# A convolution and spectral-mixing kernel: x kept on chip, mixing with stationary weights, and the kept part added in phase 3

## The chip, the cores and the metric

The kernel runs on one core of one Trainium2 chip. A core has a matrix engine (TensorE, PE in the profile, whose weight loads are listed as PEld), a vector engine (VectorE, DVE), a scalar engine (ScalarE, ACT), a general engine (GpSimd, POOL), a queue engine (SyncE, SP) and 16 DMA engines that move data between DRAM and the on-chip memory SBUF. Matrix results land in a second on-chip memory, PSUM. The metric is the device time in microseconds of one execution.

## The reference

The input x has 8 batches of 3264 positions with 192 channels, in float32. First comes a causal convolution with 7 taps, whose taps are a softmax and are shared by the 24 channels of each of 8 heads. Its result u0 goes through a spectral mixing of 64 modes, and a dense layer ends it:

```python
w = exp(weight - weight.max(-1)); w = w / (w.sum(-1) + 1e-9)
u0 = einsum('hk,bskhg->bshg', w, windows_of_7(x))
X = rfft(u0, axis=1)
Yr = einsum('bmd,mde->bme', Xr, w_r) - einsum('bmd,mde->bme', Xi, w_i)
Yi = einsum('bmd,mde->bme', Xr, w_i) + einsum('bmd,mde->bme', Xi, w_r)
y = irfft(Yr + 1j * Yi, n=S, axis=1)
u = u0 + y
out = u + maximum(u @ w_ch, 0.0)
```

Only the first 64 modes of Y are filled. w_r and w_i are 64 x 192 x 192 each.

## The kernel before

The sequence is cut into 27 windows of 122 output positions; a window needs 128 input positions (6 overlap), one per partition. `load_xw` (L73 to L81) fetches one batch into `xw` as bf16 with three DMAs that POOL issues; three such buffers exist, so batch b+2 is fetched when batch b-1 has been used.

Setup: the taps' softmax (L87 to L106), the band matrices `cband` from seven masks made by POOL (L114) and 56 DVE steps (L120, L125), and the table of cosines and sines `fstore` from a chain on DVE over 1728 elements per partition (`kprod` L144, `targ` L153 to L160) and two sines on ACT (L164, L166).

Phase 1, per batch: `conv_loop` (L300) runs, for each window and head, one matmul with the window as the stationary side (32 columns) and the band as the moving side (122 columns), L318. The result comes out transposed, channels on partitions. DVE copies four windows at a time to `cTA` and `cTB` (L329, L331), which hold the convolved sequence of all batches. `dft_and_correction` (L338) multiplies `fstore` with the unconvolved x (L343), and turns that into the spectrum of the convolved sequence by further small matmuls (L360, L363) with the operators `rop` and `cgm`; two transposes (L368, L369) and eight strided DVE copies put it into `xtA` and `xtB`.

Then 27 transposes of `fstore`, scaled by ACT, give the inverse table `gstore` (L434, L435). Mixing (L444 to L503): for each of 8 groups of 8 modes four DMAs on POOL fetch the weights (L450; two buffers of each). The spectrum is the stationary side (32 columns) and the weights are the moving side (192 columns), L479; the result is copied to `ymix` (L486), transposed (L487, L488) and copied to `yeT` (L492, L498).

`zwi` (L515 to L517) multiplies the mixed spectrum with [w_ch, identity], 384 columns. Phase 3 (L522 to L549), for each of 208 tiles of up to 128 positions: three matmuls with 384 columns accumulate [u @ w_ch, u]: L533 and L535 from the stored convolution with [w_ch, identity] (`wi`), L537 from `gstore` and `zwi`. ACT takes the Relu of the first half (L540), DVE adds the second half (L541), and SP sends three tiles with one DMA (L544; L549 for the two last tiles of a batch). `otile` has three buffers.

The framework inserts the semaphores. A buffer is reused only when its last reader is done, DMAs included. Each engine works through its own stream in order, and these streams are ordered when the program is built.

## Time and profile before

| | us |
|---|---|
| median of 3 runs (345.3 to 348.7) | 347.3 |
| span of the profiled execution | 344.8 |
| PE busy | 261.6 |
| DVE busy | 243.2 |
| ACT busy | 85.7 |
| POOL busy | 73.7 |

The profiled execution's own time is not listed apart from its span, the time from its first to its last instruction. A row of a group reads: line, engine, operation, output <- inputs, partitions x elements and type, count | busy us, mean ns of one | idle time of the engine before them and what ended it. A row of the timeline reads: start, length, engine, line, operation. "Granted clock" is the share of full TensorE clock that the chip allowed, and a DMA's time to landing runs from its issue to the arrival of its last byte. Two neighbouring matmuls overlap, so the distance of two starts is their price, not the length of one.

### The profile page before, as it was taken

To read this page: it belongs to the slowest core of one execution; us is meant where nothing else is said; L and a number is where in the kernel's file an instruction comes from. 1 tells how busy PE (TensorE), PEld (TensorE's weight loads), DVE (VectorE), ACT (ScalarE), POOL (GpSimd) and SP (SyncE) were. 2 spreads that over 40 slices of the span, in tenths; PEclk is the share of its full clock that TensorE was granted. 3 is DMA by queue.
4 is the path that set the end of the run, shared out by engine and by line. 5 is a ranking of instruction groups with operands and counts; after the bars stand their busy time and mean duration, and the time that the engine had idled before them with its cause. 6 is when DMAs were issued, how large, how long until landed. Compare 5 with 4: busy or idle time off the path is not lost.

```text
span 344.8 us, 7813 instructions
## 1 busy us (share of the span) xinstructions
PE 261.6 (76%) x3075; PEld 147.0 (43%) x3075; DVE 243.2 (71%) x700; ACT 85.7 (25%) x246; POOL 73.7 (21%) x116
## 2 busy tenths in 40 slices
PE   0232283776787895694489899889899999999985
PEld 0121251554555664431133333325465565565552
DVE  3999999999979998420064754665577676676654
ACT  3000310000000000024400000005566666666653
POOL 8869303732133000000163333000000000000000
PEclk9999999699899987655555555557999999999999
DMA  8930914999959900000099999203555555555554
GB/s 91 191 37 10 140 16 49 191 191 156 151 58 132 129 3 2 0 2 0 0 153 158 164 162 155 34 0 102 186 178 190 196 192 195 190 191 191 199 177 155
DMA packets 81172, 40.68 MB, mean 118 GB/s; under 512 B 55024, under 2 KB 81136, under 8 KB 81136
## 3 DMA queue, kind: packets, MB, share of 16 engines
q0 software_dynamic: 53600, 20.10, 50.6%
q1 hardware_dynamic: 27536, 20.09, 17.3%
q8 instruction: 24, 0.39, 0.5%
q14 instruction: 12, 0.10, 0.1%
HBM read 40.21 MB, written 20.05 MB: 175 GB/s over the span
## 4 chain that ended last, share of the span: by engine, by line
PE 43%; DVE 24%; issue 20%; DMA 7%; POOL 4%; ACT 1%; POOLq 0%; DVEq 0%; ACTq 0%
PE gps L533 9%; PE mixt L479 9%; PE gps L537 8%; PE gps L535 8%; DVE cTB L331 5%; DMA out_dram<-otile 4%; DVE cTA L329 4%; DVE cband L125 3%; DMA wiB<-in_moe_w_i_dram 2%; PE xps L343 1%; PE blk_a L318 1%; PE et L488 1%; DVE ymix L486 1%; PE et L487 1%; POOL xw L77 1%
## 5 line engine op out<-in xcount | busy, mean ns | idle before, releaser
L541 DVE TENSOR_TENSOR otile<-rz,gps 128x192 f32<-128x192 f32 x208 | 72.9, 353 | 35.7 <-ACT rz L540 8.4
L540 ACT ACTIVATE rz<-gps 128x192 f32<-128x192 f32 x208 | 68.6, 330 | 101.9 <-PE gps L537 100.1
L533 PE MATMUL gps<-wi,cTA 128*128 128x384 bf16 x208 | 69.0, 332 | 2.6 <-DVE otile L541 2.5
L537 PE MATMUL gps<-zwi,gstore 128*128 128x384 bf16 x208 | 68.6, 330 | 0.0
L535 PE MATMUL gps<-wi,cTB 128*128 128x384 bf16 x208 | 68.6, 330 | 0.0
L318 PEld LDWEIGHTS <-xw 128*32 128x32 bf16 x1728 | 32.7, 106 | 69.0 <-issue 62.6
L318 PE MATMUL blk_a<-cband,xw 128*32 128x122 bf16 x864 | 30.0, 244 | 35.5 <-DVE cband L125 14.6
L486 DVE CAST ymix<-mixt 16x192 bf16<-16x192 f32 x64 | 22.3, 352 | 31.1 <-PE mixt L479 29.2
L318 PE MATMUL blk_b<-cband,xw 128*32 128x122 bf16 x864 | 28.9, 243 | 18.4 <-DVE cTB L331 12.0
L329 DVE CAST cTA<-blk_a 128x488 bf16<-128x488 f32 (+1 forms) x56 | 36.2, 647 | 1.1 <-PE blk_a L318 1.1
L435 ACT ACTIVATE gstore<-tpsg,ascale 128x122 bf16<-128x122 bf16 (+1 forms) x27 | 9.8, 362 | 106.9 <-PE tpsg L434 106.9
L331 DVE CAST cTB<-blk_b 128x488 bf16<-128x488 f32 (+1 forms) x56 | 35.0, 626 | 0.1
L343 PE MATMUL xps<-xw,fstore 128*128 128x192 bf16 x216 | 30.0, 285 | 0.7 <-DVE fstore L168 0.7
L533 PEld LDWEIGHTS <-cTA 128*128 128x128 bf16 x208 | 20.6, 99 | 17.8 <-issue 5.7
L535 PEld LDWEIGHTS <-cTB 128*128 128x128 bf16 x208 | 20.7, 99 | 16.2 <-issue 4.3
L537 PEld LDWEIGHTS <-gstore 128*128 128x128 bf16 x208 | 20.7, 99 | 13.8 <-issue 0.7
L450 POOL DMA_DIRECT2D wrA<-in_moe_w_r_dram x8 | 7.2, 901 | 84.8 <-PE mixt L479 81.5
L343 PEld LDWEIGHTS <-fstore 128*128 128x128 bf16 x216 | 19.9, 111 | 5.8 <-issue 1.1
L479 PE MATMUL mixt<-wrA,xtA 128*32 128x192 bf16 x64 | 16.6, 333 | 5.1 <-DVE ymix L486 3.3
L479 PE MATMUL mixt<-wrB,xtB 64*32 64x192 bf16 x64 | 16.9, 341 | 0.0
L479 PEld LDWEIGHTS <-xtB 64*32 64x32 bf16 x128 | 8.4, 100 | 19.0 <-issue 18.8
L479 PEld LDWEIGHTS <-xtA 128*32 128x32 bf16 x128 | 8.6, 102 | 16.3 <-issue 12.0
(126 smaller groups left out, 286.5 us busy)
## 6 DMA issues: line engine op xcount, KB each, us to landing
out_dram<-otile SPq DMA_DIRECT2D x64, 288.0 KB, 2.3
xw<-in_x_dram POOLq DMA_DIRECT2D x8, 1200.0 KB, 11.2
wrA<-in_moe_w_r_dram POOLq DMA_DIRECT2D x8, 384.0 KB, 5.7
wiA<-in_moe_w_i_dram POOLq DMA_DIRECT2D x8, 384.0 KB, 7.7
wrB<-in_moe_w_r_dram POOLq DMA_DIRECT2D x8, 192.0 KB, 6.0
wiB<-in_moe_w_i_dram POOLq DMA_DIRECT2D x8, 192.0 KB, 7.7
out_dram<-otile SPq DMA_DIRECT2D x8, 96.0 KB, 2.1
out_dram<-otile SPq DMA_DIRECT2D x8, 48.0 KB, 1.9
```

Of the source, the lines that this page charges most:

```text
L125: nc.vector.scalar_tensor_tensor(out=cband[:, h, :], in0=maskk[:, k, :], scalar=wsb[:, h, k:k + 1], in1=cband[:, h, :], op0=ALU.mult, op1= ...
L318: nc.tensor.matmul(tconv[32 * g : 32 * g + 32, col0 : col0 + WIN], xw[:, c, xc0 : xc0 + 32], cband[:, h, :], start=True, stop=True, tile_p ...
L329: nc.vector.tensor_copy(out=cTA[:, b, s_begin : s_begin + blk_cols], in_=blk_a[:, 0:blk_cols])
L331: nc.vector.tensor_copy(out=cTB[:, b, s_begin : s_begin + blk_cols], in_=blk_b[:, 0:blk_cols])
L343: nc.tensor.matmul(xps[:, 0:D], fstore[:, c, :], xw[:, c, :], start=(c == 0), stop=(c == NWIN - 1))
L479: nc.tensor.matmul(tls[pos][r, 0:D], stat, wst[:, mj, :], start=(pi == 0), stop=(pi == len(plan) - 1), tile_position=(0, 32 * pos))
L486: nc.vector.tensor_copy(out=ymix[r, :], in_=tls[pos][r, 0:D])
L533: nc.tensor.matmul(gps[0:ns, 0:2 * D], cTA[:, b, si:si + ns], wi[:, 0, :], start=True, stop=False)
L535: nc.tensor.matmul(gps[0:ns, 0:2 * D], cTB[:, b, si:si + ns], wi[:, 1, :], start=False, stop=False)
L537: nc.tensor.matmul(gps[0:ns, 0:2 * D], gstore[:, si:si + ns], zwi[:, b, :], start=False, stop=True)
L540: nc.scalar.activation(out=rz[0:ns, :], in_=gps[0:ns, 0:D], func=ACT.Relu)
L541: nc.vector.tensor_tensor(out=otile[0:ns, t, :], in0=rz[0:ns, :], in1=gps[0:ns, D:2 * D], op=ALU.add)
```

## The change

The kernel body is rewritten.

- All of x is loaded once into `x_all` (all batches, bf16): 24 DMAs of 8 or 9 windows and one each for the first and last window of all batches, all on POOL. `perm`, a signed permutation, is built on POOL behind the loads.
- The bands: softmax on 8 partitions, the taps written to a zeroed row, the row sent to DRAM (`vdram`) and read back as 128 shifted copies, reversed by one DVE copy.
- `conv_unit`: the band is the stationary side (128 columns), up to 10 windows of one head the moving side (216 columns on average), 24 matmuls per batch. ACT copies each half of the heads over x itself in `x_all`, 48 copies in all.
- `dft` multiplies the table with the convolved sequence, so the correction, `rop`, `cgm` and `ccrm` are gone. `xtrans` transposes the 64-mode spectrum, real and imaginary parts stacked on the partitions, by six small matmuls.
- The convolved sequence is also transposed into `cT`: `t_part` makes up to 8 blocks of 122 positions in PSUM and DVE copies them at once; 6 parts per batch, 48 in all. 28 are issued in phase 1, 20 in the mixing, one per group.
- Mixing: 32 groups of 2 modes, five buffers of weights, two DMAs per group (real parts to partitions 0 to 63, imaginary to 64 to 127). The weights are the stationary side (128 columns), the spectrum the moving side (16 columns), 384 matmuls. The result has the channels on partitions already; no transposes follow.
- Phase 3: 54 groups of two windows and two batches (the last windows of four batches for two of them), 12 matmuls each: four with 384 columns, eight with 192. The Relu argument accumulates in `z`; `y` holds only the mixed part. VectorE adds the convolved sequence from `x_all` to `y`, and a second add of the Relu runs on GpSimd for two groups of three and on VectorE for the third. Four DMAs on SP send a group. `r` and `t` have three buffers each.

The trig chain is the same but for its base, and `yeT` and `zwi` (now in four pairs, scaled there) have the same use.

```diff
...
+    UNITS = ((0, 10), (10, 8), (18, 9))
+    USLOTS = ((0, 15), (15, 12), (27, 14))
...
+    x_all = constp.tile([P, B, NWIN, D], BF16, tag="x_all")
...
+    def load_mid(b, c0, n):
+        nc.gpsimd.dma_start(out=x_all[:, b, c0:c0 + n, :], in_=xwin_src(b, c0, n))
+    lastrow0 = WIN * (NWIN - 1) - OV
+    nlast = S - lastrow0
+    nc.vector.memset(x_all[0:32, :, 0, :], 0.0)
+    nc.vector.memset(x_all[96:P, :, NWIN - 1, :], 0.0)
+    load_mid(0, 1, 9)
+    nc.gpsimd.dma_start(out=x_all[OV:P, :, 0, :], in_=x[:, 0:WIN, :].rearrange("b p d -> p b d"))
+    load_mid(0, 10, 8)
+    nc.gpsimd.dma_start(out=x_all[0:nlast, :, NWIN - 1, :],
+                        in_=x[:, lastrow0:S, :].rearrange("b p d -> p b d"))
+    load_mid(0, 18, 8)
...
+    vdram = dramp.tile([H, 256], BF16, name="vdram")
...
+        nc.vector.tensor_scalar(out=vrow[:, 127:127 + KK], in0=wexp[:], scalar1=wrec[:, 0:1],
+                                scalar2=None, op0=ALU.mult)
+        nc.sync.dma_start(out=vdram[:], in_=vrow[:])
+        va = vdram[:]
+        hank = sp.tile([P, H, P], BF16, tag="hank")
+        nc.sync.dma_start(out=hank[:], in_=bass.AP(tensor=va.tensor, offset=va.offset,
+                                                   ap=[[1, P], [256, H], [1, P]]))
+        nc.vector.tensor_copy(out=cband[:], in_=hank[:, :, ::-1])
...
+    for b in range(1, B):
+        load_mid(b, 1, 9)
+        load_mid(b, 10, 8)
+        load_mid(b, 18, 8)
+    nc.gpsimd.memset(perm[:], 0.0)
+    nc.gpsimd.affine_select(out=perm[:, 0:64], in_=perm[:, 0:64], compare_op=ALU.not_equal, fill=-1.0,
+                            base=-64, pattern=[[-1, 64]], channel_multiplier=1)
...
+    wp = early_stack.enter_context(tc.tile_pool(name="wts", bufs=5, side="right"))
+    wtiles = []
+    for g in range(NGRP):
+        wt = wp.tile([P, MG, 3, D], BF16, tag="wt")
+        for half, src in ((0, moe_w_r), (1, moe_w_i)):
+            nc.gpsimd.dma_start(out=wt[64 * half:64 * half + 64, :, :, :],
+                                in_=src[MG * g:MG * g + MG, :, :].rearrange("m (p j) e -> p m j e", j=3))
+        wtiles.append(wt)
...
+    def conv_unit(b, u):
+        w0, n = UNITS[u]
+        for half in range(2):
+            cp = pconv.tile([P, 4, 256], F32, tag="cv")
+            for j in range(4):
+                h = 4 * half + j
+                nc.tensor.matmul(
+                    cp[:, j, 0:GRP * n].rearrange("p (w e) -> p w e", w=n), cband[:, h, :],
+                    x_all[:, b, w0:w0 + n, GRP * h:GRP * h + GRP], start=True, stop=True)
+            dst = x_all[0:WIN, b, w0:w0 + n, 96 * half:96 * half + 96].rearrange(
+                "p w (j e) -> p j w e", j=4)
+            srcv = cp[0:WIN, :, 0:GRP * n].rearrange("p j (w e) -> p j w e", w=n)
+            nc.scalar.copy(out=dst, in_=srcv)
...
+    def t_part(b, s0, n):
+        tp = ptr.tile([P, 8 * WIN], BF16, tag="tp")
+        for k in range(n):
+            t_slot(tp[:, WIN * k:WIN * k + WIN], b, s0 + k)
+        nc.vector.tensor_copy(out=cT[:, b, WIN * s0:WIN * (s0 + n)], in_=tp[:, 0:WIN * n])
+    def dft(b):
+        xp = pxx.tile([P, 512], F32, tag="xp")
+        for c in range(NWIN):
+            k = WIN if c < NWIN - 1 else LASTVALID
+            nc.tensor.matmul(xp[:, 0:D], fst[0:k, c, :], x_all[0:k, b, c, :],
+                             start=(c == 0), stop=(c == NWIN - 1))
...
+    def xtrans(b, xs):
+        tp = pxx.tile([P, 3, P], F32, tag="xt")
+        xsv = xs[:, :].rearrange("k (p j) -> k j p", j=3)
+        for j in range(3):
+            nc.tensor.matmul(tp[0:64, j, :], xsv[:, j, :], ident[:], start=True, stop=True,
+                             tile_position=(0, 0))
+            nc.tensor.matmul(tp[64:P, j, :], xsv[:, j, :], perm[:], start=True, stop=True,
+                             tile_position=(0, 64))
...
+    tq = []
+    pend = None
+    for b in range(B):
+        for u in range(3):
+            conv_unit(b, u)
+            if u == 0 and b > 0:
+                pend = (b - 1, dft(b - 1))
+            if u == 1 and pend is not None:
+                xtrans(*pend)
+                pend = None
+            if b < 5:
+                for _ in range(2):
+                    if tq:
+                        t_part(*tq.pop(0))
+            tq.extend(t_unit_halves(b, u))
+    xtrans(B - 1, dft(B - 1))
...
+        wt = wtiles[g]
+        for mj in range(MG):
+            m = m0 + mj
+            for t in range(2):
+                o = yps[:, t, 16 * (m % HALF):16 * (m % HALF) + 16]
+                for j in range(3):
+                    nc.tensor.matmul(o, wt[:, mj, j, 64 * t:64 * t + P], xt[:, j, m, :],
+                                     start=(j == 0), stop=(j == 2))
...
+        if gq and g % 2 == 0:
+            g_part(gq.pop(0))
+        if tq:
+            t_part(*tq.pop(0))
+    while tq:
+        t_part(*tq.pop(0))
+    early_stack.close()
+    ps1.close()
...
+    p3 = ctx.enter_context(tc.tile_pool(name="p3", bufs=3, side="right"))
+    pz = ctx.enter_context(tc.tile_pool(name="pz", bufs=2, space=PSUM))
...
+    def group(combos):
+        zp = pz.tile([P, 2, 512], F32, tag="z")
+        yp = pz.tile([P, 2, 512], F32, tag="y")
+        for k, (q, w) in enumerate(combos):
+            sa, sb, par = slot_of(w)
+            glhs = gst[:, WIN * w:WIN * w + P]
+            nc.tensor.matmul(zp[:, k, 0:2 * D], glhs, zwi[:, 0, 2 * q:2 * q + 2, :], start=True, stop=False)
+            for i in range(2):
+                b = 2 * q + i
+                o = zp[:, k, D * i:D * i + D]
+                nc.tensor.matmul(o, cT[:, b, WIN * sa:WIN * sa + P], win0[:, 0:D], start=False, stop=False)
+                nc.tensor.matmul(o, cT[:, b, WIN * sb:WIN * sb + P], wBs[par], start=False, stop=(i == 1))
+            nc.tensor.matmul(yp[:, k, 0:2 * D], glhs, zwi[:, 1, 2 * q:2 * q + 2, :], start=True, stop=True)
+        last = combos[0][1] == NWIN - 1
+        n = LASTVALID if last else WIN
+        r = p3.tile([P, 2, 2 * D], F32, tag="r")
+        t = p3.tile([P, 2, 2 * D], F32, tag="t")
+        nc.scalar.activation(out=r[0:n, :, :], in_=zp[0:n, :, 0:2 * D], func=ACT.Relu)
+        q0, w0 = combos[0]
+        tv = t[0:n, :, :].rearrange("p k (b e) -> p k b e", b=2)
+        yv = yp[0:n, :, 0:2 * D].rearrange("p k (b e) -> p k b e", b=2)
+        if last:
+            xv = x_all[0:n, 2 * q0:2 * q0 + 4, w0, :].rearrange("p (k b) e -> p k b e", k=2)
+        else:
+            xv = x_all[0:n, 2 * q0:2 * q0 + 2, w0:w0 + 2, :].rearrange("p b k e -> p k b e")
+        nc.vector.tensor_tensor(out=tv, in0=yv, in1=xv, op=ALU.add)
+        npool[0] += 1
+        eng = nc.gpsimd if npool[0] % 3 else nc.vector
+        eng.tensor_tensor(out=t[0:n, :, :], in0=t[0:n, :, :], in1=r[0:n, :, :], op=ALU.add)
+        if last:
+            dst = out[2 * q0:2 * q0 + 4, WIN * w0:WIN * w0 + n, :].rearrange("b p e -> p b e")
+            nc.sync.dma_start(out=dst, in_=t[0:n, :, :].rearrange("p k (b e) -> p (k b) e", b=2))
+        else:
+            for i in range(2):
+                dst = out[2 * q0 + i, WIN * w0:WIN * (w0 + 2), :].rearrange("(k p) e -> p k e", k=2)
+                for r0, r1 in ((0, 112), (112, WIN)):
+                    nc.sync.dma_start(out=dst[r0:r1], in_=t[r0:r1, :, D * i:D * i + D])
...
+    zwi_pair(0)
+    for q in range(B // 2):
+        for i in range(PAIRS):
+            group([(q, 2 * i), (q, 2 * i + 1)])
+            if i == 1 and q + 1 < B // 2:
+                zwi_pair(q + 1)
+        if q % 2 == 1:
+            group([(q - 1, NWIN - 1), (q, NWIN - 1)])
...
```

606 lines of the change are left out of this document (147 added, 459 removed).

## The prediction

> **What bounds the kernel now.** I read the cores first, then the busy time by stage, then the groups and the timeline.
>
> ```profile
> core 0: 344.8 us, clock 0.837
> 0.00:12.40 12.40, 0.00 (x0) 0.00 (x0) 6.50 (x30) 2.81 (x3) 11.26 (x29) 1.00 1.04 121
> 12.40:142.00 129.60, 82.60 (x2102) 59.22 (x2102) 121.85 (x314) 4.54 (x8) 43.52 (x64) 0.92 0.78 91
> 142.00:171.00 29.00, 17.59 (x80) 6.74 (x80) 4.99 (x17) 9.77 (x27) 0.00 (x0) 0.54 0.00 1
> 171.00:225.00 54.00, 48.46 (x254) 18.72 (x253) 32.11 (x126) 0.00 (x0) 18.87 (x24) 0.50 1.15 132
> 225.00:232.20 7.20, 6.91 (x16) 1.65 (x16) 4.28 (x10) 0.00 (x0) 0.00 (x0) 0.50 0.00 0
> 232.20:344.80 112.60, 106.05 (x625) 60.67 (x624) 73.50 (x209) 68.61 (x208) 0.00 (x0) 0.98 0.53 179
> ```
>
> The columns are the stretch, its length, the busy time of PE, weight loads, DVE, ACT and POOL, then granted clock, DMA share and GB/s. Each stage has its own limit. The convolution (12.4 to 142) is DVE's, 121.85 of 129.6 us. From 142 to 171 nothing is full: PE and ACT pass 27 transposes of gstore to each other one by one, and the DMA engines rest. The mixing (171 to 225) is held by PE at clock 0.50 while its weights arrive alongside. The last stage is PE's, 106 of 112.6 us. So the question is what each stage is bound by next.
>
> ```profile
> 276.00 0.33 PE L533 MATMUL gps<-wi,cTA 128*128 128x384 bf16 x1
> 276.98 0.33 PE L533 MATMUL gps<-wi,cTA 128*128 128x384 bf16 x1
> 80.72 1.66 PE L343 MATMUL xps<-xw,fstore 128*128 128x192 bf16 x18
> 100.34 0.36 PE L363 MATMUL xcps<-xs,rop 128*128 128x24 bf16 x8
> 142.09 0.23 PE L368 MATMUL xtps<-ident,xcs 128*128 128x128 bf16 x1 [0.45 <-DVE xcs L366]
> 142.25 0.24 PE L369 MATMUL xtps<-ident,xcs 128*64 128x128 bf16 x1
> 8.00:16.00 8.00, 1.41 (x37) 1.13 (x41) 8.00 (x31) 0.00 (x0) 7.71 (x23) 1.00 1.60 191
> 176.00:186.00 10.00, 9.06 (x48) 3.63 (x47) 5.05 (x20) 0.00 (x0) 3.77 (x5) 0.50 1.59 190
> ```
>
> These price PE and the loads. Between the two L533 rows lie six matmuls of 384 columns: 0.98/6 = 163 ns each. Of the 18 with 192 columns the last ends some 0.25 us after its start: (1.66-0.25)/17 = 83 ns. That makes 0.417 ns per column plus 3, the weight load hidden: 93 ns for 216 columns, 54 for 122. Eight with 24 columns and a full stationary side take (0.36-0.17)/7 = 27 ns each. The two isolated transposes start 160 ns apart, load not hidden. Loads saturate at 190 GB/s as bf16, x and mixing weights alike.
>
> **Start: the convolution begins at 16 us instead of 12.4.** The 56 DVE steps that built the bands go; the bands now travel to DRAM and back between the softmax and one reversing copy.
>
> ```profile
> 5.51 0.22 DVE L103 TENSOR_TENSOR wsb<-wexp,wrec 128x56 f32<-128x56 f32 x1
> 243.94 4.36 DMA out_dram<-otile
> out_dram<-otile SPq DMA_DIRECT2D x8, 48.0 KB, 1.9
> wiA<-in_moe_w_i_dram POOLq DMA_DIRECT2D x8, 384.0 KB, 7.7
> 22.30 1.94 DVE L144 TENSOR_TENSOR kprod<-sidx,midx 128x1728 f32<-128x1728 f32 x1
> 24.17 0.65 DVE L329 CAST cTA<-blk_a 128x488 bf16<-128x488 f32 x1
> 24.75 1.04 DVE L153 TENSOR_SCALAR targ<-kprod 128x1728 f32<-128x1728 f32 x1
> ```
>
> Softmax ends at 5.7. Each hop costs between 1.9 (smallest transfer of the output) and 7.7 (loaded queue); I take 4.4, an output landing under load. The copy of 1024 elements costs 1.2 at kprod's rate. 5.7+8.8+1.2 = 15.7; ends 10.7 and 22.3. The trig chain is unchanged. The last two rows show that DVE's stream is ordered by readiness (a copy of the convolution stands between two trig steps written ahead of it), so I let trig fill DVE while the bands travel.
>
> **Phase 1: PE 16 to 85 us.**
>
> ```profile
> L329 DVE CAST cTA<-blk_a 128x488 bf16<-128x488 f32 (+1 forms) x56 | 36.2, 647 | 1.1 <-PE blk_a L318 1.1
> L331 DVE CAST cTB<-blk_b 128x488 bf16<-128x488 f32 (+1 forms) x56 | 35.0, 626 | 0.1
> ```
>
> The 112 evictions leave DVE (36.2+35.0 = 71 us), and so do 64 strided copies to xtA and xtB. New on PE: convolution 8x24x93 ns = 17.9; dft 8x27x83 = 17.9; xtrans 48x160 = 7.7; transposes 55 per batch, 28 of the 48 parts here, so 257. Each is 54 (hidden load) to 160 ns (isolated); I take 80, nearer the hidden end since equal shapes follow each other as in the xps row: 20.6, ends 13.9 and 41.1. Sum 64, hence 80.
>
> ```profile
> L540 ACT ACTIVATE rz<-gps 128x192 f32<-128x192 f32 x200 | 66.0, 330 | 99.7 <-PE gps L537 97.9 <-DVE otile L541 1.8
> L164 ACT ACTIVATE fstore<-targ2a 128x1728 bf16<-128x1728 f32 x1 | 1.6, 1643 | 28.0 <-DVE targ2a L160 28.0
> L351 DVE COPY cct<-ccps 6x256 bf16<-6x256 bf16 x8 | 2.1, 264 | 0.0
> POOL wi L252 <- DMA xw<-in_x_dram: 3.5, 1, 3.5
> ```
>
> Beside it: ACT's slope is (1643-330)/1536 = 0.855 ns per element, so a half of 864 elements takes 0.9; 48 of them and the two sines make 46, done near 62. DVE copies 976 elements in 1.0 (L351 four times) to 1.3 (L329 twice): 28 to 36 us for 28 parts and 16 of trig. x is 10.5 MB at 190 GB/s from 4 us: all here by 59. None ends after 80. One wait is new: perm is built on POOL behind 24 loads of x, and the L252 row is POOL's thirteenth DMA held until an earlier one landed, the fifth by count. So if POOL keeps eight in flight, it frees when the eighteenth of 26 lands, 7.2 MB or 42 us, and xtrans of batch 0, with all later PE work behind it, can stand for 0 to 15 us. I add 5: 85.
>
> **Phase 2: 85 to 132.** The 29 us of gstore alone vanish (4 transposed blocks ride in the mixing), as do ymix, its zeroing and the yeT transposes. 384 matmuls at 27 ns are 10 us, 20 parts at 9.2x80 ns are 15: PE has room at full clock. The bytes stay 9.4 MB. Five of 32 groups are fetched ahead; 27x295 KB/190 = 41.9, plus 1.4 before the first refill is issued (group 0 and two issues of 0.56, next row) and about 3.5 to land, mix and copy the last group: 47. Stationary weights buy little here by themselves.
>
> ```profile
> L279 POOL DMA_DIRECT2D winat<-in_moe_w_ch_dram x1 | 0.6, 555 | 0.0
> ```
>
> By the 0.50 of the mixing stage with PE busy 48 of 54 us, PE could run this stage at half clock: transposes 160, matmuls 54 ns, 54 us in sum, 7 more. The Trainium skill (TensorE: Matmul & The Clock Gate, Part 4) says that transposes do not count as PE work for the gate; by that rule half clock holds here and the sum ends 7 us later. The 0.54 in the transposing stage agrees, but idle PE would explain that too.
>
> **Phase 3: 134.3 to 243.7.** The first zwi pair costs 4x0.43+0.56 = 2.3 (6.91/16 from the table). A group of 488 rows then costs PE 4x163+8x83 = 1.32 us, and there are 54: 71 us against 106. But its results pass through one of three t buffers.
>
> ```profile
> L541 DVE TENSOR_TENSOR otile<-rz,gps 128x192 f32<-128x192 f32 x200 | 70.3, 354 | 34.3 <-ACT rz L540 6.9 <-DMA out_dram<-otile 4.5
> 7.99 1.62 POOL L114 TENSOR_SCALAR_AFFINE_SELECT maskk<-ones_f 128x122 f32<-128x122 f32 x6
> L272 POOL MEMSET winat<- 128x768 bf16 x1 | 0.7, 737 | 0.1
> 15.13 0.35 POOL L254 TENSOR_SCALAR_AFFINE_SELECT wi<-wi 24x192 bf16<-24x192 bf16 x1
> 20.55 3.90 POOL L254 TENSOR_SCALAR_AFFINE_SELECT wi<-wi 24x192 bf16<-24x192 bf16 x1
> L544 SPq DMA_DIRECT2D out_dram<-otile x64: 372/372/402, 236.1 to 340.5; - x64
> ```
>
> VectorE add of 768: 354+576x(1940-354)/1536 = 0.95. Second add, two of three times on POOL, which no row shows: six selects of 122 elements in 1.62 are 2.2 ns per element, 1.70 for 768; ends 0.74 (memset of the same size) and, scaled from L254, 15.6. I take 1.70, the f32 row. Then four DMAs on SP at 0.37: the last starts 1.11 later and lands after 1.9. With 0.2 for the hops a buffer comes free after 0.95+1.70+1.11+1.9+0.2 = 5.86, and three groups need it: 1.95 per group. SP alone needs 1.49, DVE 0.95+0.32 = 1.27, POOL 1.13, ACT 0.82. So the buffers set the pace, PE waits, and phase 3 takes 54x1.95 = 105.5, no better than before; waits for t already show in L541's row. The last group ends 3.9 after the pace: 134.3+105.5+3.9 = 243.7.
>
> **Sum.** 16+69+47+2.3+105.5+3.9 = 243.7 against the span of 344.8; the median of the runs shown is 347.3, 2.5 above that span: **246 us**.
>
> **Rivals.** (a) The buffers return sooner: POOL's add at the memset's 0.74 gives 4.9/3 = 1.63 per group, 88 us, total 229; SP's 1.49 is the floor, 221. For it: fixed costs inside the select's row. Against: two inputs per element. (b) PE lags: transposes at 160 ns and the full wait for perm put phase 1 at 16+85+15 = 116, and half clock adds 7: 284. For it: the isolated transposes and the L252 wait. Against: hidden loads at equal shapes. (c) Slower than before: POOL is locked out by VectorE. The select of 3.90 us ran beside kprod and the last band steps on DVE; its like took 0.35. Phase 3 would need 206.6 us for no change, so 36 POOL adds above 5.7 us each decide it; at 15.6 the kernel takes about 700. Against: only every third group has a VectorE add with two SBUF inputs. The Trainium skill (SBUF — State Buffer, Who interferes with whom) makes just such instructions, and the two-port modes, lock GpSimd out; the slow select beside steps of those kinds agrees. By it the lock costs at most one 0.95 per three groups, 17 us in all.
>
> **How the numbers follow.** My forecast 0.50 (its own range 228 to 262), (a) 0.22, (b) 0.20, (c) 0.04, another way 0.04. The range of 8 in 10 reaches from (a)'s floor with phase 1 a little early, 214, to (b), 286. A measurement of this kernel tells about 1% from no change: faster 0.94, within 1% 0.02, slower 0.04.
>
> **What would show it.** Convolution at 16; the last xtrans near 85; load rate 190 GB/s without a gap through the mixing; in phase 3 VectorE's first add waiting for an output DMA in most groups, PE at two thirds, groups 1.95 us apart. Groups 1.5 apart with SP always issuing would be (a); PE busy at clock 0.5 before 100 us would be (b); POOL full in phase 3, (c). A POOL add far from 1.70 or a PE stream that waits for perm breaks the sum first.

## The result and the profile after

The kernel takes 309.1 us (median of 4 runs, 305.9 to 310.9) against 348.0 for the kernel before in the same comparison: a ratio of 0.887, 95% interval 0.878 to 0.896. The sign was right. The time, 246 with a range of 214 to 286, was not. Some executions take 1 to 2% longer than the fastest of their kernel; the ratios leave these out, and the profile of the run with five t buffers, four r buffers and four batches is of such an execution (287.3 us). First the busy time by stage of the changed kernel; the columns are those of the table before.

```profile
core 0: 308.0 us, clock 0.847
0.00:26.70 26.70, 0.00 (x0) 0.00 (x0) 9.02 (x17) 1.49 (x2) 13.00 (x18) 1.00 1.13 118
26.70:50.00 23.30, 15.76 (x101) 10.27 (x102) 11.68 (x11) 19.16 (x22) 13.78 (x12) 1.00 1.60 192
50.00:110.50 60.50, 59.51 (x630) 45.74 (x631) 32.48 (x46) 25.21 (x31) 13.27 (x25) 0.94 0.63 80
110.50:142.00 31.50, 31.05 (x344) 18.34 (x344) 13.59 (x24) 4.56 (x6) 14.28 (x24) 0.52 0.72 105
142.00:171.90 29.90, 8.81 (x239) 7.81 (x237) 3.63 (x6) 3.56 (x5) 17.74 (x30) 0.50 1.00 158
171.90:177.50 5.60, 4.19 (x17) 2.44 (x18) 0.62 (x1) 0.89 (x2) 0.00 (x0) 0.50 0.00 0
177.50:300.50 123.00, 81.72 (x648) 59.38 (x646) 71.77 (x75) 44.97 (x57) 64.81 (x36) 0.94 0.59 159
300.50:308.00 7.50, 0.00 (x0) 0.00 (x0) 0.00 (x0) 0.00 (x0) 0.00 (x0) 0.50 0.32 87
```

Set beside the terms of the prediction's sum:

| stage | predicted | measured | off by |
|---|---|---|---|
| start, to the first matmul of the convolution | 16 | 26.7 | +10.7 |
| phase 1 | 69 | 83.8 | +14.8 |
| mixing | 47 | 61.4 | +14.4 |
| first zwi pair | 2.3 | 5.6 | +3.3 |
| phase 3 | 105.5 | 123.0 | +17.5 |
| tail | 3.9 | 7.5 | +3.6 |
| span | 243.7 | 308.0 | +64.3 |

No single term carries the miss; every one is short. Each stage was then looked at by itself.

**Start and phase 1.** The timeline of the changed kernel shows which waits the start consists of (start in us, duration, engine, line, operation; in brackets the idle time before it and what ended it).

```profile
3.31 3.51 POOL L71 DMA_DIRECT2D x_all<-in_x_dram  x1
4.15 2.67 DVE L111 TENSOR_SCALAR vrow<-wexp,wrec 8x7 bf16<-8x7 f32 x1
6.85 0.27 SPq L113 DMA_DIRECT2D vdram<-vrow  x1
12.15 0.39 SPq L116 DMA_DIRECT2D hank<-vdram  x1
22.87 0.43 DVE L118 COPY cband<-hank 128x1024 bf16<-128x1024 bf16 x1 [16.05 <-DMA hank<-vdram]
23.21 1.95 DVE L127 TENSOR_TENSOR kprod<-sidx,midx 128x1728 f32<-128x1728 f32 x1
26.75 1.76 PE L208 MATMUL cp<-x_all,cband 128*128 128x240 bf16 x8 [26.75 <-DMA x_all<-in_x_dram]
46.71 3.17 ACT L143 ACTIVATE fst<-targ 128x1728 bf16<-128x1728 f32 x2
49.94 0.83 PE L247 MATMUL xp<-x_all,fst 122*128 122x192 bf16 x5 [3.92 <-ACT fst L143]
49.95 0.64 DVE L241 COPY cT<-tp 128x976 bf16<-128x976 bf16 x1 [11.62 <-issue]
```

The bands' trip to DRAM and back takes 5.3 us out (6.85 to 12.15) and 10.7 back, where 4.4 each were assumed. It also leaves late: the step before it (L111) lasts until 6.82, just as long as GpSimd's issue of the 122-row load of the first window (L71). With the reversing copy the bands are ready at 23.3. The first matmul still waits 3.4 us more, for x: that load was issued at 3.31 and takes 23.3 us to land. VectorE waits 16 us for the bands with the trig chain queued behind, although trig needs nothing of them. The order on each engine is fixed when the kernel is built, by a planner, and it need not be the written order: ScalarE's two sines, written ahead of the convolution, stand behind 18 of its copies and end at 49.9, and two things start within 0.1 us of that: the DFT, and the first copy of a transposed part into cT. Between 26.7 and 50 PE works for 15.76 of 23.3 us.

**Transposes and the mixing.** Timeline of PE, at full clock in phase 1 and at half clock in the mixing:

```profile
75.88 0.28 PE L225 MATMUL tp<-ident,x_all 122*128 122x122 bf16 x2
76.27 0.28 PE L225 MATMUL tp<-ident,x_all 122*128 122x122 bf16 x2
124.19 0.49 PE L306 MATMUL yps<-xt,wt 128*128 128x16 bf16 x12
124.86 0.39 PE L225 MATMUL tp<-ident,x_all 122*128 122x122 bf16 x2
125.42 0.39 PE L225 MATMUL tp<-ident,x_all 122*128 122x122 bf16 x2
128.21 0.49 PE L306 MATMUL yps<-xt,wt 128*128 128x16 bf16 x12
```

From one row of a pair to the next lie four transposes (two whole, two halves): 0.39/4 = 97 ns at full clock, 0.56/4 = 140 at half. Between two groups of the mixing (124.19 and 128.21) stand 3.6 us of transposes, two to three parts, not the one part that the program writes there. Weights for five groups are here, the next load starts when a group hands its buffer back, and so 110 to 142 moves 105 GB/s with PE full. Afterwards the parts are used up, PE works 8.8 of 29.9 us, and the loads come at 158 GB/s.

**Phase 3.** Groups of instructions between 177 and 300, and one turn of a t buffer in the timeline:

```profile
L377 POOL TENSOR_TENSOR t<-t,r 122x768 f32<-122x768 f32 x36 | 64.8, 1806 | 70.0 <-DVE t L374 41.6 <-DMA out_dram<-t 21.9 <-ACT r L366 6.1
L374 DVE TENSOR_TENSOR t<-yp,x_all 122x768 f32<-122x768 f32 (+1 forms) x54 | 51.4, 956 | 49.7 <-DMA out_dram<-t 33.5 <-PE yp L361 11.4 <-PE zp L360 2.8
L366 ACT ACTIVATE r<-zp 122x768 f32<-122x768 f32 (+1 forms) x54 | 43.7, 810 | 70.8 <-POOL t L377 54.7 <-PE zp L360 6.8 <-DVE t L377 5.6
```

```profile
214.92 0.96 DVE L374 TENSOR_TENSOR t<-yp,x_all 122x768 f32<-122x768 f32 x1 [1.06 <-PE zp L360]
216.01 1.81 POOL L377 TENSOR_TENSOR t<-t,r 122x768 f32<-122x768 f32 x1 [0.21 <-DVE t L374]
217.84 0.75 SPq L385 DMA_DIRECT2D out_dram<-t  x2
218.21 1.22 SPq L385 DMA_DIRECT2D out_dram<-t  x3
221.43 0.96 DVE L374 TENSOR_TENSOR t<-yp,x_all 122x768 f32<-122x768 f32 x1 [0.95 <-DMA out_dram<-t]
```

VectorE's first add waits most for an output DMA, as forecast. (The two rows of SPq share one issue; there are four.) The turn is 6.51 us here (add 0.96, POOL 1.81, then 3.6 us from the first of four issues to the next add), forecast 5.86. The first adds start from 177.5 to 298.4: 120.9/53 = 2.28 us per group, or 6.84 per turn.

### The profile page after: what moved, and what is told of

Its sections match the earlier page's. It is cut to its first block, busy times and chain, and to the rows that moved or that the text cites. A ratio compares the mean times of both kernels' runs of the same rounds, so it can differ in the third digit from the quotient of the medians.

```text
span 308.0 us, 5139 instructions
## 1 busy us (share of the span) xinstructions
PE 201.0 (65%) x1971; PEld 144.0 (47%) x1971; DVE 142.8 (46%) x174; ACT 99.8 (32%) x123; POOL 136.9 (44%) x145
## 4 chain that ended last, share of the span: by engine, by line
PE 35%; DMA 24%; POOL 12%; DVE 8%; ACT 7%; issue 6%; SPq 6%; DVEq 0%; POOLq 0%; ACTq 0%
DMA out_dram<-t 11%; POOL t L377 10%; PE tp L225 8%; DMA x_all<-in_x_dram 8%; PE tp L222 7%; PE xp L247 7%; DVE t L374 6%; SPq L385 6%; PE cp L208 5%; DMA wt<-in_moe_w_i_dram 5%; ACT x_all L214 4%; PE yps L306 2%; POOL wt L192 2%; ACT r L366 1%; PE tp L289 1%
## 5 line engine op out<-in xcount | busy, mean ns | idle before, releaser
L377 POOL TENSOR_TENSOR t<-t,r 122x768 f32<-122x768 f32 x36 | 64.8, 1806 | 70.0 <-DVE t L374 41.6
L374 DVE TENSOR_TENSOR t<-yp,x_all 122x768 f32<-122x768 f32 (+1 forms) x54 | 51.4, 956 | 49.7 <-DMA out_dram<-t 33.5
L366 ACT ACTIVATE r<-zp 122x768 f32<-122x768 f32 (+1 forms) x54 | 43.7, 810 | 70.8 <-POOL t L377 54.7
L214 ACT CAST x_all<-cp 122x960 bf16<-122x960 f32 (+2 forms) x48 | 39.0, 886 | 59.9 <-PE cp L208 59.8
L355 PE MATMUL zp<-zwi,gst 128*128 128x384 bf16 x108 | 36.7, 340 | 32.0 <-ACT r L366 28.6
L359 PE MATMUL zp<-win,cT 128*128 128x192 bf16 x216 | 48.7, 255 | 0.0
L208 PE MATMUL cp<-x_all,cband 128*128 128x240 bf16 (+2 forms) x192 | 26.7, 276 | 30.3 <-DMA x_all<-in_x_dram 26.7
L192 POOL DMA_DIRECT2D wt<-in_moe_w_r_dram x32 | 19.3, 602 | 57.7 <-PE yps L306 47.3
L359 PEld LDWEIGHTS <-cT 128*128 128x128 bf16 x216 | 21.8, 101 | 42.7 <-issue 39.6
L225 PE MATMUL tp<-ident,x_all 122*128 122x122 bf16 x216 | 36.5, 255 | 0.0
L208 PEld LDWEIGHTS <-cband 128*128 128x128 bf16 x192 | 18.5, 104 | 35.2 <-DVE targ L134 26.7
L361 PE MATMUL yp<-zwi,gst 128*128 128x384 bf16 x108 | 28.9, 343 | 4.3 <-DVE t L374 4.3
L222 PE MATMUL tp<-ident,x_all 122*64 122x122 bf16 x224 | 31.6, 274 | 0.0
L360 PEld LDWEIGHTS <-cT 128*128 128x128 bf16 x216 | 21.8, 101 | 9.9 <-issue 1.7
L360 PE MATMUL zp<-win,cT 128*128 128x192 bf16 x112 | 26.2, 257 | 0.0
## 6 DMA issues: line engine op xcount, KB each, us to landing
x_all<-in_x_dram POOLq DMA_DIRECT2D x1, 366.0 KB, 23.3
```

The source lines that it names most:

```text
L192: nc.gpsimd.dma_start(out=wt[64 * half:64 * half + 64, :, :, :], in_=src[MG * g:MG * g + MG, :, :].rearrange("m (p j) e -> p m j e", j=3))
L208: nc.tensor.matmul(cp[:, j, 0:GRP * n].rearrange("p (w e) -> p w e", w=n), cband[:, h, :], x_all[:, b, w0:w0 + n, GRP * h:GRP * h + GRP], ...
L214: nc.scalar.copy(out=dst, in_=srcv)
L222: nc.tensor.transpose(o[64 * k:64 * k + 64, :], x_all[0:WIN, b, w + k, P:D], idw, tile_position=(0, 64 * k))
L225: nc.tensor.transpose(o, x_all[0:WIN, b, w, 0:P], idw)
L355: nc.tensor.matmul(zp[:, k, 0:2 * D], glhs, zwi[:, 0, 2 * q:2 * q + 2, :], start=True, stop=False)
```

## The experiments

Each is the changed kernel with the edit named. Times are medians of 4 runs; ratios are to the kernel before, run beside each, and 0.887 (0.878 to 0.896) is the changed kernel's own.

| run | us | ratio, 95% interval |
|---|---|---|
| edge loads cut | 300.7 | 0.860 (0.855 to 0.866) |
| sines first | 317.8 | 0.911 (0.904 to 0.917) |
| sines first, perm early | 296.0 | 0.855 (0.848 to 0.863) |
| both, sines from the fifth unit | 296.5 | 0.846 (0.839 to 0.854) |
| both, sines from the third unit | 292.1 | 0.837 (0.829 to 0.845) |
| all parts in phase 1 | 313.6 | 0.899 (0.894 to 0.905) |
| six weight buffers | 305.0 | 0.881 (0.873 to 0.889) |
| parts by matmul | 304.1 | 0.869 (0.861 to 0.877) |
| parts spread, as written | 309.1 | 0.882 (0.874 to 0.890) |
| parts spread, forced | 297.9 | 0.854 (0.846 to 0.862) |
| five t buffers | 289.4 | 0.827 (0.821 to 0.834) |
| adds swapped | 295.8 | 0.857 (0.851 to 0.864) |
| four batches per group | 298.9 | 0.865 (0.861 to 0.869) |
| five t, four r, four batches | 283.8 | 0.810 (0.803 to 0.817) |
| the same, half the output | 281.4 | 0.808 (0.800 to 0.816) |
| the same, Relu added from PSUM | 284.9 | 0.820 (0.813 to 0.827) |
| all repairs | 251.4 | 0.720 (0.714 to 0.727) |
| all repairs, Relu added from PSUM | 251.0 | 0.724 (0.719 to 0.730) |

### The start

**The edge loads cut.**

```diff
-    nc.gpsimd.dma_start(out=x_all[OV:P, :, 0, :], in_=x[:, 0:WIN, :].rearrange("b p d -> p b d"))
+    for a, z in ((0, 112), (112, WIN)):
+        nc.gpsimd.dma_start(out=x_all[OV + a:OV + z, :, 0, :], in_=x[:, a:z, :].rearrange("b p d -> p b d"))
...
+    for a, z in ((0, 96), (96, nlast)):
```

> The two loads of the edge windows (122 and 98 rows) are each cut in two (112+10 and 96+2 rows). Theory: a load of 122 rows occupies few DMA engines for long, and the transfers behind it, the read-back of the bands among them, wait; cut, the bands are here near 14 us, the convolution starts at 16 to 18 instead of 26.7, and the kernel takes 299 to 302. Rival: what holds the start is the number of loads in the queue or the small transfers' own latency; then the rate between 8 and 16 us stays under 70 GB/s, the convolution starts at 25 or later, and the time stays at 307 to 311.

The first window's transfers (KB each, us to landing) in the changed kernel and with the loads cut, then the window from 8 to 12 us of both in the same order:

```profile
x_all<-in_x_dram POOLq DMA_DIRECT2D x1, 366.0 KB, 23.3
```

```profile
x_all<-in_x_dram POOLq DMA_DIRECT2D x1, 336.0 KB, 6.6
```

```profile
8.00:12.00 4.00, 0.00 (x0) 0.00 (x0) 0.00 (x0) 0.00 (x0) 4.00 (x8) 1.00 0.84 38
```

```profile
8.00:12.00 4.00, 0.00 (x0) 0.00 (x0) 0.00 (x0) 0.00 (x0) 3.52 (x5) 1.00 1.59 190
```

The same window lands after 6.6 us instead of 23.3, the rate no longer drops to 38 GB/s, the convolution starts at 19.1 instead of 26.7, and the kernel gains 8.4 us, as the theory has it. The two loads were cut together, so that the share of each is not known. What the cut does for the bands is less than the theory says. Their trip takes 5.7 and 8.7 us instead of 5.3 and 10.7 and lands at 18.6, not at 14. It leaves 2.7 us earlier (4.15), since L111 now takes 0.22 us instead of 2.67; the window of x no longer holds the first matmul, and that is 3.4 us more. The Trainium skill (DMA: Bandwidth & Descriptors, "Why a DMA increments its semaphore by 16 and not by 1") says that a transfer runs on the largest number of engines up to 16 that divides the slowest dimension of both its sides, with an exception for some copies of GpSimd's queues. Without the exception that is 2 for 122 rows and 16 for 112, an estimate from the page's rule. The two landings fit it; the engines themselves were not counted.

**The sines first.**

```diff
-        nc.vector.tensor_copy(out=cband[:], in_=hank[:, :, ::-1])
+        nc.scalar.copy(out=cband[:], in_=hank[:, :, ::-1])
...
+            tc.add_manual_dep(cvc.ins, sin_i.ins.name, NOSYNC, reason='order')
```

The added line orders each of the convolution's copies (`cvc`) behind the second sine (`sin_i`) on ScalarE; it sets only the order in which the two stand on that engine.

> The reversing copy of the bands moves from VectorE to ScalarE, and ScalarE's two sines are put ahead of the convolution's copies. Theory: VectorE's 15 us of trig wait behind the reversing copy, and the sines behind 18 copies, so that the DFT's matrix is ready at 49.9 only while PE rests for half of 27 to 50; with this order it is ready at 28 to 30, PE works on from there, phase 1 ends 8 to 11 us sooner and the kernel takes 298 to 302. Rival: PE had other work to do anyway and the limit of 27 to 50 is ScalarE's copies or x; then the time is 306 to 311.

The table was ready at 28.9 as the theory says, and yet the kernel became 9 us slower. Neither theory had it. Waits of PE (total us, times, longest):

```profile
PE tp L260 <- POOL perm L156: 14.2, 1, 14.2
```

and GpSimd's timeline in the same run:

```profile
57.95 0.88 POOL L64 DMA_DIRECT2D x_all<-in_x_dram  x1 [1.40 <-DMA x_all<-in_x_dram]
59.36 0.25 POOL L156 TENSOR_SCALAR_AFFINE_SELECT perm<-perm 128x64 bf16<-128x64 bf16 x1
```

The first transposing matmul of batch 0 now comes at 45, but perm is built at 59, behind the last load of x. This is the wait that the prediction named and priced at 0 to 15 us. In the changed kernel it costs nothing: perm is built by 58.9, and as the late sines and cT hold PE back, its first matmul with perm comes at 63.

**Perm before the loads.**

```diff
+    nc.gpsimd.memset(perm[:], 0.0)
...
     nc.gpsimd.memset(ident[:], 0.0)
```

> As the run with the sines ahead (317.8), and the permutation for xtrans is built on GpSimd before the loads of batches 1 to 7 instead of behind them. Theory: the 14.25 us that PE stood before the first matmul with perm go; the sines then save what PE rested between 27 and 50, less what it now waits at the start: 300 to 305. Rival: the next late thing (x of the next batch, ScalarE's copies) takes its place: 309 or more.

296.0, a larger gain than expected: 21.8 less than with the sines alone, or 19 by the two ratios. The mixing begins at 100.3 instead of 118.8, so 18.5 of it lie ahead of it: the 14.2 of the wait, and part of the rest is the clock, which after that pause showed 0.93 from 60 to 118 against 0.97 here from 50 to 105. The same run tells why cT was late (timeline of VectorE):

```profile
28.95 0.08 DVE L183 MEMSET cT<- 128x24 uint32 x1 [4.27 <-ACT fst L148]
```

Even cT's zeroing waits for the sines, which have nothing to do with its data. In the changed kernel (49.96), with the edge loads cut (41.16) and here it starts within 0.1 us of their end. The trig's pool is closed before cT's is opened, so that the two can share memory. That this is the reason was not tested by separating them.

**Both repairs.** The cut loads and the run above together, the sines ahead of the copies from the fifth unit of the convolution on, then from the third:

```diff
+            if (b, u) >= (1, 1): tc.add_manual_dep(cvc.ins, sin_i.ins.name, NOSYNC, reason='order')
...
+            if (b, u) >= (0, 2): tc.add_manual_dep(cvc.ins, sin_i.ins.name, NOSYNC, reason='order')
```

> The edge loads cut in two, the reversing copy on ScalarE, the sines ahead of the copies from the fifth unit of the convolution on, perm built early. Theory: the gain of the cut edges (8) and that of the order (13) add up less what both counted, since each takes the same waits at 16 to 27 and 40 to 50: 285 to 292. Rival: x, which lands at 190 GB/s until 47 to 57, becomes the limit of phase 1: 293 to 297.

> As the run with both repairs of the start (296.5), the sines ahead of the copies from the third unit on instead of the fifth. Theory: there the sines ended at 34.3, and until then both the DFT and the first copy of a transposed part into cT (whose memory the trig used before) stood; trig is done at 24.5, so the sines end at 28 to 29, PE does not stand at 30 to 34, and the kernel takes 286 to 291. Rival: x of the next batch or ScalarE's copies hold PE in their place: 294 to 297.

The first missed (296.5): the sines ended at 34.3, and DFT and cT stood until then. From the third unit on the kernel takes 292.1, just outside the 286 to 291 expected; the mixing begins at 94.4 against 98.6. The direction is the theory's, but the intervals of the two ratios overlap, and so the gain of this step alone is not settled.

### The mixing

**All parts in phase 1.**

```diff
-            if b < 5:
+            if b < 8:
...
+    while tq:
+        t_part(*tq.pop(0))
     xtrans(B - 1, dft(B - 1))
```

> All 48 transposed parts stand in phase 1, none in the mixing. Theory: in the mixing's first half PE is full at half clock with the transposes and sends back the weight buffers late; without them the mixing is the loads' (45 to 50 us instead of 61.4), while phase 1 grows by 20 x 9.2 x 0.097 = 18 us at full clock: 309 to 316 in all. Rival: the latency of a load with five buffers sets the mixing, parts or not: it stays at 58 or more, 322 to 328 in all.

313.6 in all, in the theory's range, though its ratio overlaps the changed kernel's. From its first matmul to the first of zwi the mixing now takes 48.1 us, and phase 1 pays for it. That window:

```profile
130.20:178.30 48.10, 15.70 (x396) 13.84 (x396) 5.69 (x8) 6.86 (x10) 32.03 (x54) 0.51 1.03 167
```

The mixing without parts thus takes about the predicted 47, at half clock and with PE busy for a third of the time; the parts between the groups make the other 13.

**Six weight buffers.**

```diff
-    wp = early_stack.enter_context(tc.tile_pool(name="wts", bufs=5, side="right"))
+    wp = early_stack.enter_context(tc.tile_pool(name="wts", bufs=6, side="right"))
```

> Six buffers for the mixing's weights instead of five. Theory: after the transposes are done, the five loads in flight over their latency give the 158 GB/s of 142 to 171.9; six give 185 to 190, 4 to 5 us less, and one group more is there ahead of the stage, 1 to 2 us: 301 to 305. Rival: GpSimd's issue or PE's return of the buffers sets the rate: 307 to 311.

305.0 lies at the end of the expected range, but the ratios overlap: no difference that this measurement settles. In the profiled execution the mixing takes 55.8 us (109.1 to 164.9) instead of 61.4, about what the theory asks for.

**Parts by ordinary matmuls,** in the mixing only.

```diff
-                nc.tensor.transpose(o, x_all[0:WIN, b, w, 0:P], idw)
+                nc.tensor.matmul(o, x_all[0:WIN, b, 2 * i + r, 0:P], ident[0:WIN, 0:WIN], start=True, stop=True)
```

> The 20 parts that stand in the mixing are turned by ordinary matmuls against the identity (f32 in PSUM, four slots to a bank, twice as many copies) instead of TensorE transposes; those of phase 1 stay. Theory: the clock is 0.52 in a stretch in which PE is 99% busy because transposes do not raise it; with matmuls it rises to 0.8 or more in the first half of the mixing, that half takes 22 to 27 us instead of 31.5, the kernel 300 to 305. Rival: it is the 16-column matmuls, which wait for weight loads, that leave it at half; the clock stays at 0.5 to 0.6 and the time at 306 to 313.

304.1, inside the theory's range, but not for its reason. The clock in windows of this run, all parts turned by ordinary matmuls (the last transposes, of the DFT's table, end at 121):

```profile
125.00:130.00 5.00, 4.59 (x54) 2.69 (x52) 3.43 (x6) 0.00 (x0) 2.45 (x5) 0.50 1.01 147
130.00:135.00 5.00, 4.84 (x52) 2.71 (x51) 4.02 (x7) 0.71 (x1) 2.38 (x4) 0.50 0.95 127
```

From 125 on no transpose is left, PE is busy 92 to 97%, and the clock is 0.50, as the rival has it. Over 110 to 142 it is 0.61 against 0.52, since it drops later, and the loads run at 140 GB/s against 105, as the planner placed the parts differently; the gain was not split between the two. The Trainium skill (TensorE: Matmul & The Clock Gate, Part 4) says that transposes don't count as work for the gate; here half clock stays without them, so that rule alone does not explain it. The rival's 16-column matmuls were not taken away in any run, and the kernel before showed 0.50 in its mixing with 192 moving columns. The cause was not found.

**Parts spread over the groups.** Once as the program writes it, once with each part ordered behind its group's last matmul on PE.

```diff
-        if tq:
+        if tq and g % 3 != 2:
...
+        if tq and g % 3 != 2:
+            with tc.issue_after(mm.ins): t_part(*tq.pop(0))
```

> The 20 parts are spread over two of three of the mixing's 32 groups instead of one in each of the first 20. Theory: the first half of the mixing is PE's (31.05 of 31.5 us) while the loads rest, the second is the loads' while PE rests (8.8 of 29.9); mixed evenly, both run side by side and the 61.4 us become 48 to 54: 295 to 302. Rival: a group that holds a part sends its weight buffer back late wherever it stands; 304 to 310.

> As the earlier spread (two of three of the 32 groups), but each part is ordered behind the last mixing matmul of its group on PE, so that the planner can't pull it forward. Theory: the first half of the mixing is PE's with 2 to 3 parts between two groups while the loads rest, the second the loads' while PE rests; truly even, the 61.4 us become 47 to 54 and the kernel takes 294 to 302. Rival: with parts among the groups to the end each weight buffer goes back late (five in all), the loads run at 110 to 140 GB/s throughout: 304 to 312.

The first run decides nothing: the planner pulled the parts to the front again, and VectorE's copies stand at the same times as before (the last at 142.1 against 141.5). Forced, the mixing lasts 49.3 us (112.4 to 161.7) and the kernel takes 297.9: the theory holds.

```profile
112.40:142.00 29.60, 25.95 (x385) 17.09 (x384) 10.88 (x18) 5.26 (x7) 22.77 (x39) 0.52 1.08 171
142.00:161.70 19.70, 13.23 (x205) 8.62 (x204) 6.34 (x11) 2.85 (x4) 9.27 (x16) 0.50 0.94 152
```

The clock is still at half, and PE has time to spare (39.2 us busy of 49.3). The uneven order cost the 12 us, not the clock.

### Phase 3

**Five t buffers.**

```diff
+    p3t = ctx.enter_context(tc.tile_pool(name="p3t", bufs=5, side="right"))
...
-        t = p3.tile([P, 2, 2 * D], F32, tag="t")
+        t = p3t.tile([P, 2, 2 * D], F32, tag="t")
```

> Five t buffers instead of three, r stays at three. Theory: the turn of a t buffer (6.5 to 6.8 us for add, add, four issues, landing) over three buffers is the 2.28 us of a group; over five it is 1.35, so that SP (4 x 0.38) or PE (1.51) sets the pace at 1.5 to 1.7: the last stage takes 82 to 92 us instead of 123, the kernel 268 to 279. Rival: the r buffers or POOL's add of 1.81 take over at once, 2.0 us or more per group: 293 to 309.

289.4: between the two. The first adds come every 1.88 us (177.9 to 277.6) instead of 2.28. That the t buffers set the pace is shown. What holds it then was not isolated; the longest wait is ScalarE's for an r buffer, until GpSimd's add has read it (41 us).

**The adds swapped.**

```diff
-        nc.vector.tensor_tensor(out=tv, in0=yv, in1=xv, op=ALU.add)
...
+        eng.tensor_tensor(out=rv, in0=rv, in1=xv, op=ALU.add)
+        nc.vector.tensor_tensor(out=tv, in0=yv, in1=rv, op=ALU.add)
```

> The two adds change places: r = r + x first (GpSimd two of three times, else VectorE), then t = y + r on VectorE; three buffers each as before. Theory: a t buffer is then held only for one VectorE add, four issues and the landing (0.96 + 1.5 + 2.3 + hops = 5.0), 1.65 per group over three; GpSimd's 1.81 has gone from t's turn to r's (0.81 + 1.81 + 0.96 = 3.6, 1.2 per group). The last stage takes 88 to 98 us instead of 123, the kernel 274 to 286. Rival: adds on GpSimd and VectorE hinder each other and the three engines still pass r on in lock step, as with five t buffers (1.87 per group): 287 to 297, or no gain at all.

295.8, near the rival: 2.00 per group. The waits for output DMAs of the engines that write t fall from 55 us (VectorE 33.5, GpSimd 21.9) to 8, but ScalarE then waits 47 us for r.

**Four batches of one window per group,** two DMAs instead of four.

```diff
-            group([(q, 2 * i), (q, 2 * i + 1)])
...
+            group([(2 * hq, w), (2 * hq + 1, w)])
```

> A group of the last stage takes four batches of one window instead of two batches of two windows, so that its output needs two DMAs (112 and 10 rows, four batches each) instead of four; buffers as before. Theory: two issues of 0.38 go from the turn of a t buffer, 6.8 becomes 6.0, 2.0 per group instead of 2.28: 291 to 297. Rival: the landing grows with the size of the transfer by as much (2.3 becomes 3 or more): 304 to 310.

298.9: 2.07 per group, a turn of 6.2. Two issues less are 0.6 us less per turn, where 0.8 was expected; the time lies just above the theory's 291 to 297.

**Together, with four r buffers,** and from there two steps on: half the output left out, and in every third group the Relu added straight from PSUM.

> Five t buffers, four r buffers and two output DMAs per group (four batches of one window). Theory: with t and r no longer in short supply PE's 1.51 per group, or the adds that GpSimd and VectorE slow for each other, set the pace: 1.55 to 1.75 per group, the last stage 84 to 95 us instead of 123, the kernel 268 to 281. Rival: the stage is the output's; at the 189 GB/s of the run with five t buffers the 20 MB take 106 us whatever the buffers: 286 to 292.

```diff
-            nc.sync.dma_start(out=dst[r0:r1], in_=t[r0:r1, :, :].rearrange("p k (b e) -> p (k b) e", b=2))
+            nc.sync.dma_start(out=dst[r0:r1, 0:2], in_=t[r0:r1, 0, :].rearrange("p (b e) -> p b e", b=2))
```

> As the run with five t, four r buffers and two DMAs per group (283.8), but only the first two of each group's four batches are written out: half the output is left out. Theory: the last stage is held by the output's bytes (196 GB/s there); with half of them it falls from 97 to 88 us or less: 268 to 275. Rival: the adds and their passing between ScalarE, GpSimd and VectorE hold it: 280 to 285.

```diff
+            nc.vector.scalar_tensor_tensor(out=t[0:n, :, :], in0=zp[0:n, :, 0:2 * D], scalar=0.0,
+                                           in1=t[0:n, :, :], op0=ALU.max, op1=ALU.add)
```

> As the run with five t, four r buffers and two DMAs per group (283.8); in every third group VectorE adds max(z, 0) to t straight from PSUM in one instruction, so that it has no add with two SBUF operands and ScalarE no relu there. Theory: that add, 0.96 alone and 1.7 to 2.3 beside GpSimd's, waits until GpSimd's add is over, and its wait passes on to the next groups; reading PSUM it takes 0.96 to 1.0, PE's 1.51 sets the pace at 1.52 to 1.62 instead of 1.78, and the kernel takes 271 to 277. Rival: any second add on VectorE is slowed beside GpSimd's, or the passing between the engines holds the pace: 281 to 285.

The first gave 283.8 and 1.78 per group, just outside its theory. With half the bytes the pace is the same 1.77 (176.3 to 270.3): less output alone does not help, and DMA at 196 GB/s was no sign that it would. But VectorE is busy for 55.5 of 60 us there (200 to 260), 48.7 with the whole output, so its slow adds may have taken the place of another limit. VectorE's second add in these three runs (min/median/max in ns), in their order:

```profile
L374 DVE TENSOR_TENSOR t<-t,r x18: 955/1708/2346, 184.4 to 275.1; 122x768 f32<-122x768 f32 x16, 92x768 f32<-92x768 f32 x2
```

```profile
L374 DVE TENSOR_TENSOR t<-t,r x18: 1171/2342/2350, 180.8 to 271.4; 122x768 f32<-122x768 f32 x16, 92x768 f32<-92x768 f32 x2
```

```profile
L376 DVE SCALAR_TENSOR_TENSOR t<-zp,t x18: 953/957/958, 181.5 to 274.2; 122x768 f32<-122x768 f32 x16, 92x768 f32<-92x768 f32 x2
```

With two SBUF operands it takes up to 2.35 us beside GpSimd's adds, of 1.81 each; reading one operand from PSUM it takes 0.957 or within 0.004 of it every time. That much of the theory is right. But the pace stayed, 1.81 per group, and the time too: 284.9. In its place came a ring between PE and ScalarE (waits of the last run, 185 to 272):

```profile
ACT r L367 <- PE zp L360: 59.4, 32, 2.6
DVE t L372 <- PE yp L361: 25.4, 41, 1.9
PE zp L355 <- ACT r L367: 19.2, 29, 1.0
```

A z buffer in PSUM is now held through VectorE's two adds in every third group, and there are two. That this is what holds the pace was argued, not tested. Whether the slow add or something else set the 1.78 thus stays open.

### All repairs together

> Together: cut edge loads, reversing copy on ScalarE, sines early, perm early, six weight buffers, parts spread by force, five t and four r buffers, four batches per group with two DMAs, the last output of 92 rows cut in 80 and 12. If the gains add up (20 in start and phase 1, 8 to 12 in the mixing, 25 to 28 in the last stage and its tail), the kernel takes 248 to 258. If they hide one another: 262 to 275.

> The run with all repairs (251.4) and the add of the run before it in this list. Theory: the same 8 to 13 us: 238 to 244. Rival: 249 to 253.

251.4 us, 0.720 (0.714 to 0.727) of the kernel before and, 251.4/309.1, 0.81 of the changed one. The gains add up: 17.0 (start and phase 1), 11.2 (parts spread) and 25.3 (last stage) by themselves make 53.5, and with the sixth weight buffer and the cut last output 57.7 were reached. The Relu from PSUM adds nothing here either (251.0). Windows of the first of these two:

```profile
0.00:19.30 19.30, 0.00 (x0) 0.00 (x0) 13.42 (x21) 2.54 (x3) 16.62 (x26) 1.00 1.24 147
19.30:94.00 74.70, 71.48 (x720) 54.63 (x721) 37.74 (x49) 44.82 (x52) 22.89 (x33) 1.00 1.06 133
94.00:142.00 48.00, 39.03 (x587) 25.56 (x586) 17.32 (x28) 8.12 (x11) 30.89 (x52) 0.52 1.01 162
142.00:147.40 5.40, 5.25 (x22) 3.00 (x23) 1.24 (x2) 1.32 (x3) 0.00 (x0) 0.54 0.00 0
147.40:243.00 95.60, 75.86 (x644) 56.55 (x642) 80.65 (x74) 44.53 (x56) 63.52 (x36) 1.00 0.74 200
243.00:250.00 7.00, 0.00 (x0) 0.00 (x0) 0.00 (x0) 0.00 (x0) 1.62 (x1) 0.50 0.55 147
```

The mixing needs 48 us where 47 were predicted, phase 1 74.7 where 69 were. The start, at 19.3, still does not reach 16. Phase 3, at 95.6, beats the predicted 105.5 with more buffers and two output DMAs per group instead of four, which the prediction did not have.

## Why the prediction was wrong, by its own steps

- **Start, 16 us: the hop was mis-sized, and a wait was left out.** "I take 4.4, an output landing under load" became 5.3 and 10.7, and with the edge loads cut 5.7 and 8.7: the way back is above even the 7.7 given as the upper end. Why it is so slow stays open. The sum also knows only the bands; when they were ready, at 23.3, the first matmul had to wait until 26.7 for the first window of x, whose load of 122 rows took 23.3 us. Cutting the edge loads gave back 7.6 of the 10.7 us, mostly by this wait and an earlier departure of the bands, and little by a shorter trip.
- **Phase 1: "I let trig fill DVE while the bands travel" failed.** The order is fixed when the kernel is built; the reversing copy stands ahead of trig, and the sines behind 18 copies. The rows of the old kernel showed one such order, not that an engine picks what is ready. PE stood 8.5 us (83.8 less 15.8 and 59.5 busy). With the sines and perm early phase 1 took 73.0 (27.3 to 100.3).
- **Phase 1: the transpose at 80 ns was mis-sized;** it is 97 at full clock, 4.4 us more on 257. PE's busy time was 75.3 instead of 64, and with all repairs still 71.5; the clock (0.94 from 50 to 110.5) is another part, and the rest was not divided up.
- **Phase 1: perm.** The wait is real, 14.2 us where the sines are early, and hidden where they are not; the 5 added for it did not appear in the changed kernel. What hid it, the late table, was not in the list, and perm itself was ready at 58.9, not at 42.
- **Mixing: 47 us was the loads' share, and right for that** (48.1 and 49.3 with the parts elsewhere or spread). What failed is "PE has room": the parts were taken to lie one to a group, and the planner packed two to three between groups, which held back the weight buffers. Half clock, priced at 7 us in the prediction, did come (0.52, 0.50), but PE's work was 39.9 us there and not 54, and once the order was even the mixing took 49.3 at half clock. The rule of the Trainium skill (TensorE: Matmul & The Clock Gate, Part 4) that gave half clock agrees with the changed kernel's clock; that half clock also stood from 125 to 135 without transposes, at 0.50, shows that they are not what it takes.
- **zwi and tail** were short by 3.3 and 3.6. The pair itself took 2.8 us (171.9 to 174.75), at half clock and with its two evictions one after the other. The other 2.8 are the first group's matmuls up to VectorE's first add, which the sum put at nothing. The last output, of 92 rows, was issued at 301.3 and ended the kernel at 308.0, where 1.9 from issue to landing had been taken; cut in 80 and 12 rows with all repairs, the last issue came 3.7 us before the end.
- **Phase 3: the mechanism was right, the turn too small.** t buffers return late, PE works two thirds of the time (81.7 of 123), VectorE waits for the output. 5.86 became 6.51 in the turn shown and 6.84 on the mean: POOL's add is 1.81 instead of 1.70 (a good estimate), the issues and the landing took 3.6 instead of 3.0 in that turn, and the rest of the mean is waits that were not divided up. Rival (a) did not happen. Of (b), PE lagging, the half clock and slower transposes came, but the price lay elsewhere.
- **Rival (c), a lock between VectorE and GpSimd, is seen, the other way round:** VectorE's add is the longer one, and GpSimd's stay at 1.81 with few exceptions (at most 2.56). In the changed kernel it hardly shows: the 18 adds have a median of 0.96. The Trainium skill (SBUF — State Buffer, Who interferes with whom) says that a VectorE instruction with two SBUF inputs contends and one with a single SBUF input does not; 2.34 and 0.957 us, the medians with half the output and with the Relu from PSUM, agree.

The rivals were each tried as the whole answer. The misses of every stage had one sign: most terms were worked out as if their engine never waited for another's work, and the others from prices that were too small.

## What to carry to other kernels

Before counting on one engine's spare time, read in what order its instructions really stand: the early sines, the early perm and the spread parts change nothing but an order (and the engine of one copy), and the parts that were only written apart stood together again in the built kernel. Repair waits in pairs: the early sines alone lost 9 us until perm was early too, and five t buffers passed the wait on to r. Look at the row counts of the first transfers: cutting those of 122 and 98 rows into 112 and 10, 96 and 2 was worth 8 us here.

## What the runs showed of the hardware

- A transfer of 122 rows took 23.3 us, and one of 112 of these rows 6.6 (the 98-row transfer behind it was cut too). A VectorE step on 8 x 7 elements lasted 2.67 us, until GpSimd had issued the 122 rows, and 0.22 with the loads cut; why was not tested.
- PE had half clock (0.50) with ordinary matmuls alone and 92 to 97% busy; in phase 1 of the changed kernel it had 0.94 at 98% busy. The cause is not known.
- VectorE's add of two SBUF operands took 0.96 us alone and 2.34 beside GpSimd's adds (1.81 each), and 0.957 with one operand in PSUM, in a stage with the same adds on GpSimd.
